# Score matmuls that read neighbouring columns and write PSUM with a step, and projections held to the second products of an attention and two-layer FFN kernel

## The chip, the cores and the metric

The kernel runs on one core of one Trainium2 chip. The metric is the time of the program on the device in microseconds (us), as the median of several runs.

## The reference, cut to what matters

```python
def _attn_ref(q, k, v):                       # (4, 8, 576, 64), fp32
    q_lm = q.reshape(B, H, 32, S // 32, D).mean(axis=3)   # 32 landmarks, each the mean of 18 rows
    k_lm = k.reshape(B, H, 32, S // 32, D).mean(axis=3)
    A = sm(q, k_lm); Bm = sm(q_lm, k_lm); C = sm(q_lm, k)  # softmaxes of scaled scores
    Z = ...                                   # six steps Z = 2 * Z - Z @ Bm @ Z
    return A @ Z @ C @ v

x = attention as (2304, 512)
h = x @ w_in;  g = h * tanh(softplus(h));  x = g @ w_out       # 512 -> 2048 -> 512
h = x @ w_in2; g = h * sigmoid(h);         return g @ w_out2
```

## The kernel before, in words

Attention is worked in eight groups of four heads (`Group`, two groups for each of the four batch elements, paired by `Pair`). A group loads q and k, turns them on TensorE into `tT["q"]` and `tT["k"]` (tiles `Tq` and `Tk`), and forms the landmarks `lmT`. Group 1 keeps its turned q and k in borrowed `wp` buffers, so its rows are named `wp`. Then `scores` (L1187) makes eight matmuls for k (called from `c_side`, L1237) and eight for q (called from `a_side`, L1304): fp32, 64 rows by 32 stationary columns, 288 moving columns, each into its own 32 partitions of one of two PSUM banks, so that eight small tiles of the array work at once. `tT` holds, for each partition, `[J2 = 9, HG = 4, LM = 32]`: the 32 columns of one head and one j lie side by side, and the next j of the head is 128 columns (512 bytes) on. The two calls read it in another order: q with j innermost (`p l j`), k with c innermost (`p w l c`, three j apart, 1,536 bytes), so that the scores come out in PSUM side by side in the order in which the softmax, the 32x32 transposes and the later products use them.

What comes out of a pair is `ut`, from C @ v and the six steps. With it, `projection(b, fb)` folds the attention's right side into `w_in`: eight fp32 matmuls of 512 columns (`t<-wa,ut`) into two `t` banks, from which ACT casts the high part `wp` and DVE subtracts for the low part. The first layer then is `emit_h` (first products, `h<-at,wp`, six matmuls of 288 columns into one of two `h` banks), `gated` (ACT takes Mish out of the `h` bank as `z`, casts `g`; DVE or POOL subtracts for its low part) and `emit_o` (second products, `y<-g,wo`, twelve matmuls). A product with fp32 exactness is three fp32r passes over high and low parts. The second layer (`second_layer`, 384 columns at a time, seven products where eight stood) follows.

The order of the instructions is made by the program itself before it runs: `Line` holds a model of the engines' times, chains such as `projections` are generators that yield the engine they wait for, and the main loop (L1575) takes the next `emit_o` or `emit_h` and lets due chains issue between their matmuls (`line.run()`). `projections` runs ahead of the first products as far as three `wp` buffers allow. `grown` (L1572) is 0 while groups are still being worked on, and 1 from the time all eight are done. Every engine then takes its instructions in the fixed order that results. Where the model finds TensorE idle before `grown`, the loop adds small transposes of `ident`.

Of the kernel before, what the change touches and what calls it, by code (L numbers as in the profile page):

```python
# [61 lines left out]
def f32(ap):  # L62
    return ap.bitcast(FP32)
# [347 lines left out]
def kernel(  # L411
# [15 lines left out]
    LM = 32  # L427
    J = S // LM
    J2 = J // 2
    SH = S // 2  # L430
    HG = 4
    GB = H // HG
    NG = B * GB
    VI = S // 96
    VC = 96 // LM
# [25 lines left out]
    def slots(n, of, **kw):  # L461
# [30 lines left out]
        out=twice.rearrange("p (a d) -> p a d", a=2),  # L492
# [18 lines left out]
    def until(cond):  # L511
        while not cond():
            yield "W"

    def marked(*m):
        return lambda: all(a in marks for a in m)
# [135 lines left out]
    t_r = Ring("t", ps_t, 2)  # L652
# [12 lines left out]
    def at_of(b):  # L665
        if b not in a_t:
            a_t[b] = at_p.tile([128, 2, GB, 2, SH], F32R, tag=f"at{b}", name=f"at{b}")
        return a_t[b]

    def projections():  # L670

        for half in range(2):
            for b in range(B):
                yield from until(marked(*((b, "ut", e) for e in range(GB))))
                for fb in (2 * half, 2 * half + 1):
                    yield from projection(b, fb)

    def projection(b, fb):
        keys = [("a", 0, fb * KD + kk) for kk in range(KD)]
        parts = 1 if fb or b else 2  # L680
        n = FB // parts
        yield from until(wp_r.any)
        for c in range(0, FB, n):
            done = [k if parts == 1 else (*k, c) for k in keys]
            yield from until(lambda: all(w_ready.get(k, LATE) <= line.now for k in done))
            yield from until(lambda: t_r.claim(GB))
            pp = [t_r.take([128, FB], FP32) for e in range(GB)]
            for i in range(HG):
                for e in range(GB):
                    r = slice(64 * ((i + e) % 2), 64 * ((i + e) % 2) + 64)  # L690
                    T.matmul(
                        out=pp[e][0][32 * i:32 * i + 32, 0:n],
                        lhsT=ut_t[b][r, e, i // 2, :],
                        rhs=f32(w_t[keys[2 * e + i // 2]])[r, c:c + n],
                        start=True,
                        stop=True,
                    )
            if not c:
                wp_ = wp_t[b, fb] = wp_r.take([128, 2, GB, FB], F32R)
                wp = wp_[0]  # L700
            yield "W"
            for e in range(GB):
                VA.copy(out=wp[:, 0, e, c:c + n], in_=pp[e][0][:, 0:n])
            yield "V"
            for e in range(GB):
                V.tensor_tensor(
                    out=wp[:, 1, e, c:c + n], in0=pp[e][0][:, 0:n], in1=f32(wp[:, 0, e, c:c + n]), op=ALU.subtract
                )
                Ring.give(pp[e])
            for f in range((fb * FB + c) // 128, (fb * FB + c + n) // 128):  # L710
                wp_ready[b, f] = line.end + 0.12 + SLACK
            yield "W"
        marks.add(("P", b, fb))
# [257 lines left out]
    def emit_h(ph, t, f):  # L971
        h = h_t[ph, t, f] = h_r.take([128, 512], FP32)
        n = tokens(ph, t)[1]
        b, e = divmod(t, 2)
        wp, at = wp_t[b, f // 4][0], a_t[b]
        ops = [(wp[:, i, k, f % 4 * 128:f % 4 * 128 + 128], at[:, j, k, e]) for k in range(GB) for i, j in PASSES]
        for i, (w, x) in enumerate(ops):
            T.matmul(out=h[0][:, :n], lhsT=w, rhs=x, start=(i == 0), stop=(i == len(ops) - 1))
            if i % STRIDE == STRIDE - 1:
                yield  # L980
# [126 lines left out]
    class Group:  # L1107
# [76 lines left out]
            yield "W"  # L1184
            marks.add((g, "T" + nm))

        def scores(self, i, mov):  # L1187
            s = [self.pairs.take([128, 512], FP32) for e in range(2)]
            for r in range(2):
                for h in range(HG):  # L1190
                    e = (h + r) % 2
                    T.matmul(
                        out=s[e][0][32 * h:32 * h + 32, 0:SH],
                        lhsT=self.lmT[64 * e:64 * e + 64, i, 32 * h:32 * h + 32],
                        rhs=mov(e, h),
                        start=True,
                        stop=True,
                    )
            return s, [x[0][:, 0:SH] for x in s]
# [37 lines left out]
        def c_side(self):  # L1237
            g = self.g
            yield from until(marked((g, "lmT"), (g, "Tk")))
            yield from until(lambda: self.pairs.open(2))  # L1240
            kT = self.tT["k"]
            s_, s_c = self.scores(
                1, lambda e, h: kT[64 * e:64 * e + 64, :, h, :].rearrange("p (c w) l -> p w l c", c=VC)
            )
            marks.add((g, "sc"))
            yield "V+"
            nm2 = s_p.tile([128, 2], FP32, tag="nm2", name="nm2")
            for e in range(2):
                V.tensor_reduce(out=nm2[:, e:e + 1], in_=s_c[e], axis=AX.X, op=ALU.max)
            yield "V"  # L1250
            nmc = s_p.tile([128, 1], FP32, tag="nmc", name="nmc")
            V.tensor_reduce(out=nmc, in_=nm2, axis=AX.X, op=ALU.max, negate=True)
            yield "A+"
            e_c = a_p.tile([128, 2, SH], FP32, tag="ec", name="ec", bufs=2)
            scr = s_p.tile([128, 1], FP32, tag="scr", name="scr")
            scm = s_p.tile([128, 1], FP32, tag="scm", name="scm")
            sc2 = s_p.tile([128, 2], FP32, tag="sc2", name="sc2")
            for e in range(2):
                A.activation(out=e_c[:, e], in_=s_c[e], func=ACTF.Exp, bias=nmc, accum_out=sc2[:, e:e + 1])
                Ring.give(s_[e])  # L1260
            line.add(self.total(scm, sc2, scr), self.kind("N"), "V", line.end + 0.17)
            yield "T+"
            yield from until(lambda: g == 0 or (g - 1, "cv") in marks)
            ect = a_p.tile([96, VI, 128], FP32, tag="ect", name="ect")
            for i0 in (0, 3):
                yield from until(self.banks.open)
                pe = self.banks.take([96, 3, 128], FP32)
                for i in range(i0, i0 + 3):
                    T.transpose(
                        out=pe[0][:, i - i0, :], in_=e_c[:, i % 2, 96 * (i // 2):96 * (i // 2) + 96], identity=ident  # L1270
                    )
                yield "W"
                VA.copy(out=ect[:, i0:i0 + 3, :], in_=pe[0])
                Ring.give(pe)
                yield "T+"
            yield from until(self.banks.open)
            pu_ = self.banks.take([128, D], FP32)
            pu = pu_[0]
            for i in range(VI):
                for h in range(HG):  # L1280
                    T.matmul(
                        out=pu[32 * h:32 * h + 32],
                        lhsT=ect[:, i, 32 * h:32 * h + 32],
                        rhs=self.vn[:, h, i, :],
                        start=(i == 0),
                        stop=(i == VI - 1),
                    )
            marks.add((g, "cv"))
            yield "V"
            yield from until(lambda: ("w", scr.name) in line.seen)  # L1290
            VAs.scaled(out=self.pair.yu[:, self.hg, LM:], in_=pu, scalar1=scr)
            Ring.give(pu_)
            yield "W"
            marks.add((g, "u"))
# [9 lines left out]
        def a_side(self):  # L1304
# [1 line left out]
            yield from until(marked((g, "lmT"), (g, "Tq"), (g, "sc")))  # L1306
            yield from until(lambda: self.pairs.open(2))
            qT = self.tT["q"]
            s_, s_a = self.scores(0, lambda e, h: qT[64 * e:64 * e + 64, :, h, :].rearrange("p j l -> p l j"))
            marks.add((g, "scores"))  # L1310
            if g == 1:
                for t_ in self.borrowed:
# [241 lines left out]
    line.add(attention(), "C")  # L1554
    line.add(loading(), "S")
    line.add(projections(), "X")
    line.add(inputs(), "S")
    line.add(summed(), "S")
# [7 lines left out]
    def o_time(u):  # L1566
        ph, t, f, first, last = u
        if first and not y_r.any_of(KD):
            return LATE
        return max(g_ready.get((ph, t, f), LATE), w_ready.get(("o", 0, f), LATE))  # L1570

    grown = 0  # L1572
    todo, flight = list(units), []
    idle = 0
    while todo or flight:  # L1575
        rank_decodes(*(flight[0] if flight else todo[0]))
        line.run()
        if not grown and marked(*((g, "done") for g in range(NG)))():

            grown = 1  # L1580
# [27 lines left out]
        to = o_time(flight[0]) if flight else LATE  # L1608
        th = h_time(todo[0]) if todo and len(flight) < FLIGHT else LATE
        if to <= line.now:  # L1610
            u = flight.pop(0)
            work = emit_o(*u)
        elif th <= line.now:
            u = todo.pop(0)
            flight.append(u)
            work = emit_h(*u[:3])
        else:
# [11 lines left out]
            assert idle < 20000, (line.now, todo[:1], flight[:1], [c[4].__name__ for c in line.chains], marks)  # L1629
            continue  # L1630
        idle = 0
        ph, t, f, first, last = u
        hs = work.__name__ == "emit_h"
        for _ in work:
# [54 lines left out]
```

## Time and profile before

| | us |
|---|---|
| median of 3 runs (lowest, highest) | 836.97 (835.3 to 837.58) |
| the profiled execution | 837.15 |
| its span, first to last instruction | 835.3 |
| TensorE matmuls busy | 811.0 |
| VectorE (DVE) busy | 557.7 |
| ScalarE (ACT) busy | 432.7 |
| GpSimd (POOL) busy | 114.5 |

The span is what the trace covers; 1.85 us of the profiled execution lie around it. Rows that read "t<-Tk,lmT x16" count two records for each fp32 matmul. In a timeline row the second number is the length from the first start to the last end of a merged run of instructions; matmuls are pipelined, so the next row starts before that end, and the step from one row's start to the next row's start is what a run occupies. The number in brackets is idle time of the engine just before the row and what ended it. Almost all operations are recorded at L262, the helper that issues them, so they are told apart by tiles.

### The profile page before, as it was taken

To read this page: it belongs to the slowest core of one execution; us is meant where nothing else is said; L and a number is where in the kernel's file an instruction comes from. 1 tells how busy PE (TensorE), PEld (TensorE's weight loads), DVE (VectorE), ACT (ScalarE), POOL (GpSimd) and SP (SyncE) were. 2 spreads that over 40 slices of the span, in tenths; PEclk is the share of its full clock that TensorE was granted. 3 is DMA by queue.
4 is the path that set the end of the run, shared out by engine and by line. 5 is a ranking of instruction groups with operands and counts; after the bars stand their busy time and mean duration, and the time that the engine had idled before them with its cause. 6 is when DMAs were issued, how large, how long until landed. Compare 5 with 4: busy or idle time off the path is not lost.

```text
span 835.3 us, 15167 instructions
## 1 busy us (share of the span) xinstructions
PE 811.0 (97%) x5866; PEld 722.3 (86%) x5866; DVE 557.7 (67%) x1192; ACT 432.7 (52%) x959; POOL 114.5 (14%) x157
## 2 busy tenths in 40 slices
PE   8799999999999999999998999999999999999997
PEld 6487888978989898989998888988888988988885
DVE  6978847647657698863638999677555567555542
ACT  4467636649556656452445655435544435544422
POOL 2000200201000001000001122211232211223210
PEclk9999999999999999999999999999999999999999
DMA  8875012311034645551125232102200000100002
GB/s 276 260 181 165 29 58 87 115 51 36 31 101 162 215 159 192 185 162 50 50 85 193 75 101 90 38 1 79 73 1 2 1 1 28 48 1 1 1 0 77
DMA packets 41736, 72.28 MB, mean 87 GB/s; under 512 B 3776, under 2 KB 31936, under 8 KB 41664
## 3 DMA queue, kind: packets, MB, share of 16 engines
q1 hardware_dynamic: 40768, 70.53, 26.5%
q8 instruction: 46, 0.75, 0.4%
q10 hardware_dynamic: 896, 0.79, 0.3%
q14 instruction: 26, 0.21, 0.1%
HBM read 57.15 MB, written 14.16 MB: 85 GB/s over the span
## 4 chain that ended last, share of the span: by engine, by line
PE 86%; DVE 6%; ACT 3%; DMA 2%; issue 1%; ACTq 0%; SPq 0%; DVEq 0%
PE y L262 47%; PE h L262 31%; PE t L262 8%; DMA wp<-in_q_dram 1%; ACT z L262 1%; DVE m L262 1%; DVE wa L262 1%; ACT L262 1%; ACT wp L262 1%; DVE at L262 1%; DMA wst<-in_moe_w_out_dram 1%; DVE wo L262 0%; ACT ec L262 0%; DVE bd L262 0%; DVE yu L262 0%
## 5 line engine op out<-in xcount | busy, mean ns | idle before, releaser
L262 PE MATMUL y<-g,wo 128*128 128x288 f32 x1536 | 226.1, 299 | 0.9 <-DVE g L262 0.9
L262 PEld LDWEIGHTS y<-g,wo 128*128 128x128 f32 x1536 | 208.3, 188 | 13.8 <-issue 11.7
L262 PE MATMUL y<-wo,xg 128*128 128x512 f32 x693 | 179.8, 394 | 0.0
L262 PEld LDWEIGHTS y<-wo,xg 128*128 128x128 f32 x693 | 128.4, 188 | 20.9
L262 DVE TENSOR_TENSOR z<-h,z 128x384 f32<-128x384 f32 x160 | 87.3, 555 | 70.4 <-PE h L262 68.0
L262 PE MATMUL h<-at,wp 128*128 128x288 f32 x768 | 122.8, 302 | 4.7 <-ACT z L262 4.0
L262 PEld LDWEIGHTS h<-at,wp 128*128 128x128 f32 x768 | 105.9, 188 | 17.6 <-issue 9.6
L262 ACT ACTIVATE z<-h 128x288 f32<-128x288 f32 x128 | 51.4, 415 | 55.9 <-PE h L262 55.4
L262 DVE TENSOR_TENSOR g<-z,g 128x288 fp32r<-128x288 f32 x121 | 53.9, 462 | 31.3 <-ACT g L262 28.2
L262 ACT ACTIVATE z<-z 128x384 f32<-128x384 f32 x93 | 48.9, 525 | 32.2 <-DVE z L262 32.0
L262 PE MATMUL h<-xg,wp 128*128 128x384 f32 x288 | 57.8, 335 | 0.0
L262 ACT CAST g<-z 128x288 fp32r<-128x288 f32 x122 | 50.9, 438 | 11.1 <-PE y L262 10.0
L262 PE MATMUL h<-xg,wf 128*128 128x384 f32 x282 | 56.5, 335 | 0.0
L262 DVE TENSOR_TENSOR xg<-z,xg 128x384 fp32r<-128x384 f32 x74 | 41.9, 566 | 20.1 <-ACT xg L262 20.0
L262 PEld LDWEIGHTS h<-xg,wp 128*128 128x128 f32 x288 | 51.3, 188 | 3.2
L262 PEld LDWEIGHTS h<-xg,wf 128*128 128x128 f32 x282 | 50.2, 188 | 3.1
L262 DVE SCALAR_TENSOR_TENSOR m<-wst,m 128x512 int32<-128x512 int32 x64 | 45.3, 712 | 0.7
L262 PE MATMUL y<-wo,wp 128*128 128x512 f32 x171 | 44.9, 394 | 0.0
L262 DVE TENSOR_TENSOR wp<-t,wp 128x512 fp32r<-128x512 f32 (+1 forms) x34 | 20.8, 654 | 28.7 <-ACT wp L262 28.7
L262 ACT CAST xg<-z 128x384 fp32r<-128x384 f32 x74 | 38.0, 513 | 1.6
L262 PEld LDWEIGHTS y<-wo,wp 128*128 128x128 f32 x171 | 31.7, 188 | 5.2
L262 POOL TENSOR_TENSOR g<-z,g 128x288 fp32r<-128x288 f32 x7 | 6.3, 898 | 216.3 <-ACT g L262 112.7
(227 smaller groups left out, 1137.2 us busy)
## 6 DMA issues: line engine op xcount, KB each, us to landing
wst<-in_moe_w_out_dram SPq DMA_DIRECT2D x32, 512.0 KB, 6.6
wst<-in_moe_w_in_dram SPq DMA_DIRECT2D x22, 512.0 KB, 5.5
kn<-in_k_dram SPq DMA_DIRECT2D x8, 576.0 KB, 5.6
vn<-in_v_dram SPq DMA_DIRECT2D x8, 576.0 KB, 7.0
yh<-ysb SPq DMA_DIRECT2D x32, 144.0 KB, 2.4
ysb<-yh SPq DMA_DIRECT2D x32, 144.0 KB, 2.7
ys<-ysb SPq DMA_DIRECT2D x32, 144.0 KB, 2.1
qn<-in_q_dram SPq DMA_DIRECT2D x7, 576.0 KB, 4.8
```

The lines of the kernel that those rows point to most:

```text
L262: r = getattr(self.nc[e], name)(**kw)
```

## The change

Two edits. First, both score calls read `tT` in its stored order, 32 neighbouring columns at a time, and `scores` gets a function `to` that gives the output the step that the read had: for k the columns land three floats apart (12 bytes), for q nine floats apart (36 bytes). The values and their places in PSUM are the same. Second, once `grown` is set, a projection may begin only while the unit of the main loop is an `emit_o`; the flag `between` is set for each unit before its matmuls are issued.

```diff
+    grown, between = 0, [False]
+
     def projections():
...
             yield from until(lambda: all(w_ready.get(k, LATE) <= line.now for k in done))
-            yield from until(lambda: t_r.claim(GB))
+            yield from until(lambda: (not grown or between[0]) and t_r.claim(GB))
...
-        def scores(self, i, mov):
+        def scores(self, i, mov, to):
...
-                        out=s[e][0][32 * h:32 * h + 32, 0:SH],
+                        out=to(s[e][0][32 * h:32 * h + 32, 0:SH]),
...
             s_, s_c = self.scores(
-                1, lambda e, h: kT[64 * e:64 * e + 64, :, h, :].rearrange("p (c w) l -> p w l c", c=VC)
+                1,
+                lambda e, h: kT[64 * e:64 * e + 64, :, h, :].rearrange("p (c w) l -> p c w l", c=VC),
+                lambda s: s.rearrange("p (w l c) -> p c w l", l=LM, c=VC),
             )
...
-            s_, s_a = self.scores(0, lambda e, h: qT[64 * e:64 * e + 64, :, h, :].rearrange("p j l -> p l j"))
+            s_, s_a = self.scores(
+                0, lambda e, h: qT[64 * e:64 * e + 64, :, h, :], lambda s: s.rearrange("p (l j) -> p j l", j=J2)
+            )
...
-    grown = 0
...
         idle = 0
+        between[0] = work.__name__ == "emit_o"
```

On TensorE, in the part of the program where a group's scores stand between products of the first layer (here group 4; `Tk` and `Tq` are the turned k and q), the difference of the two orders reads:

```order
-L262 MATMUL t<-Tk,lmT 32x288 x8
+L262 MATMUL t<-Tk,lmT 32x3x96 x8
 L262 MATMUL y<-g,wo 128x288 x20
 L262 MATMUL h<-at_1187,wp 128x288 x6
 L262 MATMUL y<-g,wo 128x288 x2
-L262 MATMUL t<-Tq,lmT 32x288 x8
+L262 MATMUL t<-Tq,lmT 32x9x32 x8
```

Nothing moved there; the output of the same matmuls now has two dimensions. Up to the end of the groups the two programs have the same matmuls in the same order on TensorE.

On TensorE after the last group, where the projections of batch element 2 (`ut_143`) and 3 (`ut_144`) stand among the first layer's products, the program before has:

```order
L262 MATMUL y<-g,wo 128x288 x36
L262 MATMUL h<-at_1187,wp 128x288 x8
L262 MATMUL t<-wa,ut_143 32x512 x8
L262 MATMUL h<-at_1187,wp 128x288 x22
L262 MATMUL y<-g,wo 128x288 x2
L262 MATMUL t<-wa,ut_144 32x512 x8
L262 MATMUL y<-g,wo 128x288 x58
```

and the changed one, at the same place:

```order
L262 MATMUL y<-g,wo 128x288 x36
L262 MATMUL h<-at_1187,wp 128x288 x30
L262 MATMUL y<-g,wo 128x288 x2
L262 MATMUL t<-wa,ut_143 32x512 x8
L262 MATMUL y<-g,wo 128x288 x22
L262 MATMUL t<-wa,ut_144 32x512 x8
L262 MATMUL y<-g,wo 128x288 x36
```

The projection that cut a run of 30 first products after 8 of them now stands after the run, two second products later, and the next one stands two units of second products behind it.

## Rows read from the trace of the kernel before

**Rows 1.** The page: busy by engine, and the last chain's shares.

```profile
PE 811.0 (97%) x5866; PEld 722.3 (86%) x5866; DVE 557.7 (67%) x1192; ACT 432.7 (52%) x959; POOL 114.5 (14%) x157
...
PE 86%; DVE 6%; ACT 3%; DMA 2%; issue 1%; ACTq 0%; SPq 0%; DVEq 0%
```

**Rows 2.** Stretches: start:end, length, PE, PEld, DVE, ACT, POOL busy, clock, DMA.

```profile
60.00:110.00 50.00, 48.77 (x514) 41.58 (x514) 42.77 (x99) 29.33 (x61) 6.21 (x7) 1.00 0.34 113
110.00:232.00 122.00, 119.48 (x1220) 102.47 (x1208) 73.86 (x187) 74.70 (x161) 11.81 (x14) 1.00 0.19 60
...
436.00:460.00 24.00, 21.43 (x142) 20.32 (x141) 18.72 (x41) 11.98 (x26) 3.14 (x4) 1.00 0.58 192
```

**Rows 3.** TensorE groups, shapes apart: count, busy us, mean ns of one.

```profile
L262 PE MATMUL t<-Tq,lmT 64*32 64x288 f32 x96 | 8.9, 760 | 0.0
...
L262 PE MATMUL t<-Tk,lmT 64*32 64x288 f32 x96 | 5.5, 500 | 0.0
...
L262 PE MATMUL t<-wa,ut 64*32 64x256 f32 x32 | 1.9, 388 | 0.4 <-ACT Tk L262 0.4
```

**Rows 4.** TensorE timeline around one group's scores: start, length, instruction.

```profile
123.01 0.88 PE L262 MATMUL t<-Tk,lmT 64*32 64x288 f32 x16
123.82 2.92 PE L262 MATMUL y<-g,wo 128*128 128x288 f32 x20
...
127.72 1.40 PE L262 MATMUL t<-Tq,lmT 64*32 64x288 f32 x16
129.06 1.19 PE L262 MATMUL y<-g,wo 128*128 128x288 f32 x7
```

**Rows 5.** TensorE timeline around a projection of 256 columns.

```profile
44.51 0.66 PE L262 MATMUL t<-wa,ut 64*32 64x256 f32 x16
45.10 1.09 PE L262 MATMUL y<-ident 128*128 128x128 f32 x8
```

**Rows 6.** TensorE timeline around two projections of 512 columns.

```profile
312.91 1.09 PE L262 MATMUL t<-wa,ut 64*32 64x512 f32 x16
313.93 0.81 PE L262 MATMUL h<-at,wp 128*128 128x288 f32 x4
315.53 2.67 PE L262 MATMUL h<-at,wp 128*128 128x288 f32 x18 [0.79 <-ACT z L262]
...
318.39 1.09 PE L262 MATMUL t<-wa,ut 64*32 64x512 f32 x16
319.41 1.87 PE L262 MATMUL y<-g,wo 128*128 128x288 f32 x12
```

**Rows 7.** ScalarE timeline at the first of these two.

```profile
314.09 1.07 ACT L262 CAST wp<-t 128x512 fp32r<-128x512 f32 x2 [2.45 <-PE t L262]
315.05 0.73 ACT L262 ACTIVATE z<-h 128x288 f32<-128x288 f32 x2
```

**Rows 8.** Waits of TensorE from 225 to 460: us in total, times, longest.

```profile
PE h L262 <- ACT z L262: 3.2, 5, 0.8
PE h L262 <- DVE z L262: 1.4, 1, 1.4
```

**Rows 9.** TensorE timeline, three other places of the first of these waits.

```profile
285.68 1.58 PE L262 MATMUL h<-at,wp 128*128 128x288 f32 x10 [0.54 <-ACT z L262]
...
372.36 1.84 PE L262 MATMUL h<-at,wp 128*128 128x288 f32 x12 [0.29 <-ACT z L262]
...
400.17 2.00 PE L262 MATMUL h<-at,wp 128*128 128x288 f32 x13 [0.80 <-ACT z L262]
```

**Rows 10.** Chain of work from 36 to 42, by line.

```profile
by line: DVE wa L262 56.1%; DVE m L262 15.6%; PE t L262 12.8%; DVE at L262 6.3%; DVE wp L262 5.7%; issue 4.2%
```

**Rows 11.** Waits of VectorE from 12 to 36: us in total, times, longest.

```profile
DVE nm L262 <- PE y L262: 1.5, 2, 1.0
```

**Rows 12.** Chain of work by line, 60 to 110, then 110 to 232.

```profile
by line: PE y L262 29.5%; PE t L262 29.2%; PE h L262 10.5%; ACT L262 5.8%; DVE wo L262 4.9%; DVE m L262 3.5%; issue 2.6%; DVE wp L262 2.4%; ACT m L262 2.3%; DVE bd L262 1.8%; ACT z L262 1.7%; DVE a_t L262 1.4%; ACT at L262 1.4%; ACT eb L262
...
by line: PE y L262 38.8%; PE t L262 28.4%; PE h L262 16.6%; ACT L262 2.1%; DVE lmk L262 1.9%; DVE lmq L262 1.9%; issue 1.7%; DVE nm L262 1.4%; DVE bd L262 1.2%; DVE at L262 1.1%; ACT ec L262 1.1%; ACT wp L262 0.9%; DVE g L262 0.8%; ACT z L2
```

## The prediction

> **What bounds the kernel now.** I read the page first. TensorE is busy for 97% of the span and carries 86% of the chain that ended last [rows 1], so a microsecond taken from TensorE can reach the end, but only in stretches where TensorE does not then wait for another engine. So I cut the span into stretches and looked at the chain of waits in each. From 110 to 232 TensorE is idle for 122 - 119.5 = 2.5 us, and its three tiles (y, t, h) carry 38.8 + 28.4 + 16.6 = 84% of the chain [rows 2, 12]. From 60 to 110 VectorE is busy for 42.8 of 50 us and TensorE's share of the chain is 29.5 + 29.2 + 10.5 = 69% [rows 2, 12]. Before that the chain is VectorE's: from 36 to 42 its decoding of weights (wa, m) alone is 72%, TensorE 13% [rows 10]. After 225 TensorE's waits are few and have a pattern, 3.2 us in five waits of first products for ScalarE's z [rows 8].
>
> **Edit one, the scores: what they cost now.** Each of the eight groups issues one batch for k and one for q, eight matmuls (16 records) each. The reader should compare two batches of equal work: from its start to the next row's start k occupies 123.82 - 123.01 = 0.81 us, q 129.06 - 127.72 = 1.34 us [rows 4]. Single records differ likewise, 500 ns against 760 [rows 3]. The columns, the tile shapes and the output are alike; what differs is the order in which the moving operand is read. So reading order costs time here.
>
> What such a batch takes when the read is side by side and the write too is shown by the projections, which use the same 64x32 tiles, 16 records: 256 columns occupy 45.10 - 44.51 = 0.59 us [rows 5], 512 columns 313.93 - 312.91 = 1.02 us [rows 6]. For 288 columns that gives, as an estimate between these rows, 0.59 + (32/256) x 0.43 = 0.64 us. If the stepped write is free, a k batch gains 0.81 - 0.64 = 0.17, a q batch 1.34 - 0.64 = 0.70, a group 0.87, and eight groups 7.0 us.
>
> **What the write with a step costs** no row shows: every TensorE row of before writes neighbouring columns. The bounds: from below nothing, since 0.64 us is already the rate of matmuls that read and write side by side, and a stepped write has nothing less to do. From above, the widest step on a read that the trace has: a batch of 1.34 us for both. I take nothing, being the nearer to the rows: a k read whose step is three times q's (1,536 against 512 bytes) costs only a quarter of what q's does (0.17 against 0.70), so a step is not dear by its width alone, and the steps of the writes are 12 and 36 bytes.
>
> The Trainium skill, "PSUM — Partial Sum Buffer", section "Specifications (TRN2)", speaks against the edit: it gives PSUM lines of 8 bytes and says that any non-contiguous access pattern slows matmuls significantly. No run shows this yet; by it the gain of the scores would shrink, vanish or turn round. It is weighed as a rival.
>
> **How much of the 7.0 us reaches the end.** Groups 4 to 7 have their scores after 110, where I pass on TensorE's 84% of the chain: 4 x 0.87 x 0.84 = 2.9. Groups 2 and 3 have theirs before it: 2 x 0.87 x 0.69 = 1.2. Groups 0 and 1 come first, ahead of a stretch that VectorE's queue bounds; between nothing (its queue is full anyway) and the 1.5 us that VectorE waited there for the score banks to take their maximum (nm) [rows 11]. I take 0.8, the middle. Sum 4.9 us, 70% of 7.0. Nothing else is issued: matmuls, their count, the filler transposes and the readers' patterns stay, so no transfer or cast is added.
>
> **Edit two, the projections.** Ten projections start after 225; six of them cut a run of first products. What the cut does is read at 313 [rows 6, 7]: ScalarE's queue is in order, and the two casts of wp, planned there, wait for the projection's last matmul until 314.09 and then take 0.96 us; the Mish of an h bank stands behind them at 315.05, and as there are only two h banks, TensorE stands idle 0.79 us before its next first products. The same occurs at 285 and 400 [rows 9] and once more between them: of the 3.2 us in five waits [rows 8], 0.29 at 372 [rows 9] follows no projection closely, and I expect one of its kind to stay. Removed: 3.2 - 0.3 = 2.9 us. The projection itself costs the same between second products: 319.41 - 318.39 = 1.02 us against 1.02 in the h run [rows 6]. Where the casts wait now, TensorE has 22 to 58 second products of at most 0.15 us each to do (20 of them take 2.92 us [rows 4]), some 3 to 8 us against the 0.96 us of casts, so no h bank is needed in that time. The cover ends where, as once in the new order, a projection stands right before first products; then up to 0.8 us returns. I charge 0.3 and count 2.6 us. Later projections make wp later, by about 3 us, but a wp made when a buffer comes free is first read eight units later, and a unit is 18 products of that length, so some 20 us: hidden.
>
> Sum: 837.15 - 4.9 - 2.6 = 829.65 on the profiled execution, which stands 0.18 above the median: **829.5 us**.
>
> **The rivals.**
> *Absorbed.* The scores gain less because the step costs a little or VectorE does not follow. A batch of 0.90 us for both saves 2.15 - 1.80 = 0.35 a group, 8 x 0.35 x 0.70 = 2.0, with the projections 4.6: 832.4. For it speaks VectorE's 86% from 60 to 110 [rows 2]; against it the small idle time of TensorE after 110. VectorE absorbing groups 0 to 3 altogether leaves 2.9 + 2.6 = 5.5: 831.5.
> *The step costs as much as q's read did.* Both batches 1.34 us: k loses 0.53, q gains nothing, 8 x 0.53 x 0.70 = 3.0 lost, 2.6 won by the projections: 837.4, no change. For it speaks that a step on the read, of whatever width, cost something in both orders; against it, that the steps here are 14 times narrower and more than those. By the rule of the Trainium skill quoted above this rival or the next is what happens; no run shows it yet.
> *The step costs more, slower.* Twice q's excess on both batches, 0.64 + 1.40 = 2.04 us: 8 x (4.08 - 2.15) x 0.70 = 10.8 lost, less 2.6: 845. It becomes slower than no change can explain when 8 x 0.70 x (two batches - 2.15) exceeds 2.6 + 2.5, that is from 1.53 us a batch on. For it speaks that no row has such a write; against it, that the write would then cost 1.53 - 0.64 = 0.89 us a batch, more than the 0.70 of the dearest read.
> *The projections bring nothing.* The casts now stand ahead of second products' g casts or another z, and waits of the same size come back: 837.15 - 4.9 = 832.3 or, with one VectorE wait more at the change of layers (1.4 us at 458 now [rows 8], in a stretch where VectorE is busy 18.7 of 24 us [rows 2]), 833.6. The order of that stretch is replanned too, and its 24 - 21.4 = 2.6 us of idle TensorE may shift either way by 1 to 2 us; I add nothing.
>
> **How the numbers follow.** No change can be told apart within about 0.3%, 2.5 us: 834.5 to 839.5. Forecast as above, 826 to 831.4: 0.50. Absorbed, 831.4 to 834.5: 0.22. Projections without effect: 0.05. Step as dear as q's read, 834.5 to 839.5: 0.14. Step dearer: 0.09. The most that could be won is 7.0 + 2.9 + the 1.4 at 458 = 11.3, 825.9. So faster 0.76, same 0.15, slower 0.09. The range takes the first three cases and the better half of the fourth: 825.9 to 837.
>
> **What the profile of the changed kernel would show.** Right, if k and q batches both step by about 0.64 us and their records last near 410 ns (500 less half of the k batch's 170); if first products wait for z after 225 once at most, under 0.5 us in all; and if TensorE's idle time from 60 to 232 stays under 6 us. The step is dear if q's record does not fall clearly under k's old 500 ns, or if k's rises. Absorbed, if batches fall as said and TensorE's waits for VectorE between 60 and 110 grow by over 1 us. The forecast falls altogether with a batch over 1.1 us, or with waits of more than 2 us that stand behind the moved casts or at the change of layers.

## The result and the profile after

| | before | after |
|---|---|---|
| median of 5 runs (lowest, highest), us | 836.97 (835.3 to 837.6) | 827.56 (825.96 to 828.59) |
| after / before, 95% interval | | 0.9887 (0.9868 to 0.9906) |
| the profiled execution, its span, us | 837.15, 835.3 | 827.56, 825.6 |

The change makes the kernel 1.13% faster, about 9.4 us; 829.5 was predicted, 825.9 to 837 as the range. Beside the experiments below the kernel before ran 27 times more, with medians of 836.14 to 836.20; measured on those, the gain is about 8.6 us. The page of the changed kernel says, in its list of engines:

```profile
PE 803.1 (97%) x5866; PEld 723.1 (88%) x5866; DVE 556.8 (67%) x1194; ACT 430.6 (52%) x956; POOL 117.1 (14%) x158
```

TensorE has the same 5866 instructions and 7.9 us less to do [rows 1]. By shape (count, busy us, mean ns of one) the score records are now alike:

```profile
L262 PE MATMUL t<-Tq,lmT 64*32 64x288 f32 x96 | 4.8, 415 | 0.0
...
L262 PE MATMUL t<-Tk,lmT 64*32 64x288 f32 x96 | 4.6, 415 | 0.0
```

They were 760 and 500 [rows 3]. TensorE's timeline at the same group's two batches:

```profile
118.46 0.72 PE L262 MATMUL t<-Tk,lmT 64*32 64x288 f32 x16
119.10 2.89 PE L262 MATMUL y<-g,wo 128*128 128x288 f32 x20
...
122.98 0.71 PE L262 MATMUL t<-Tq,lmT 64*32 64x288 f32 x16
123.62 1.58 PE L262 MATMUL y<-g,wo 128*128 128x288 f32 x10
```

From start to next start both take 0.64 us, where [rows 4] has 0.81 and 1.34. In the stretches (length, busy time of PE, PEld, DVE, ACT and POOL, granted clock, DMA) TensorE's idle time from 60 to 232 is 1.40 + 3.17 = 4.57 us, and was 1.23 + 2.52 = 3.75 [rows 2]:

```profile
60.00:110.00 50.00, 48.60 (x517) 41.85 (x515) 41.06 (x96) 29.55 (x62) 6.21 (x7) 1.00 0.27 91
110.00:232.00 122.00, 118.83 (x1239) 104.47 (x1238) 77.08 (x195) 78.08 (x169) 11.69 (x14) 1.00 0.19 60
...
436.00:460.00 24.00, 22.15 (x119) 20.99 (x118) 22.04 (x48) 14.63 (x31) 4.38 (x6) 0.93 0.35 116
```

The last of these rows has something that the kernel before did not have there: a granted clock under 1.00. It comes back below. Where the two projections stood at 313 and 318 [rows 6], the changed kernel has:

```profile
304.97 4.48 PE L262 MATMUL h<-at,wp 128*128 128x288 f32 x30
309.29 0.43 PE L262 MATMUL y<-g,wo 128*128 128x288 f32 x2
309.65 1.09 PE L262 MATMUL t<-wa,ut 64*32 64x512 f32 x16
310.67 3.21 PE L262 MATMUL y<-g,wo 128*128 128x288 f32 x22
313.81 1.09 PE L262 MATMUL t<-wa,ut 64*32 64x512 f32 x16
314.82 5.07 PE L262 MATMUL y<-g,wo 128*128 128x288 f32 x36
```

No bracket, so no wait that the trace shows. A projection still occupies 1.02 and 1.01 us. TensorE's waits from 225 to 460 (total, times, longest) are now:

```profile
PE h L262 <- DVE z L262: 1.9, 1, 1.9
PE h L262 <- ACT z L262: 1.8, 3, 1.0
```

Five waits for ScalarE's z have become three, 3.2 us have become 1.8; the wait for VectorE's z at the change of layers has grown from 1.4 to 1.9 [rows 8].

To see where the 9.7 us of span went I read, in each trace, the starts of four instructions: the first scores of k; the last small product of the groups (`t<-bd,yu`); the first product of the second layer (`h<-x,wf`); the third product of the second layer that reads `x`. The table gives the first of them and then the time from each to the next, the last column to the end of the span:

| us | first scores | to the groups' end | to the second layer | change of layers | rest |
|---|---|---|---|---|---|
| before | 12.91 | 217.12 | 220.47 | 25.14 | 359.66 |
| after | 11.79 | 210.86 | 216.68 | 26.65 | 359.62 |
| difference | 1.12 | 6.26 | 3.79 | -1.51 | 0.04 |

The first 1.12 us are not the change's: the load of group 1's q landed 8.35 us after its issue in the one trace and 7.23 us in the other, and over all ten kernels of this study, with the old scores or the new, the first scores start anywhere from 11.7 to 13.0. In this execution the two edits bring 6.26 and 3.79, and at the change of layers this execution lost 1.51 us again.

### The profile page after: what moved, and what is told of

Its sections match the earlier page's. It is cut to its first block, busy times and chain, and to the rows that moved or that the text cites. A ratio compares the mean times of both kernels' runs of the same rounds, so it can differ in the third digit from the quotient of the medians.

```text
span 825.6 us, 15175 instructions
## 1 busy us (share of the span) xinstructions
PE 803.1 (97%) x5866; PEld 723.1 (88%) x5866; DVE 556.8 (67%) x1194; ACT 430.6 (52%) x956; POOL 117.1 (14%) x158
## 4 chain that ended last, share of the span: by engine, by line
PE 86%; DVE 5%; ACT 3%; DMA 3%; issue 2%; ACTq 0%; SPq 0%
PE y L262 47%; PE h L262 32%; PE t L262 8%; DMA wst<-in_moe_w_out_dram 1%; DMA wp<-in_q_dram 1%; DVE wa L262 1%; ACT L262 1%; DVE at L262 1%; ACT z L262 1%; DMA wst<-in_moe_w_in_dram 0%; DVE wo L262 0%; DVE bd L262 0%; DVE yu L262 0%; DVE z L262 0%; DVE m L262 0%
## 5 line engine op out<-in xcount | busy, mean ns | idle before, releaser
L262 DVE TENSOR_TENSOR z<-h,z 128x384 f32<-128x384 f32 x166 | 90.6, 555 | 70.5 <-PE h L262 68.2
L262 PE MATMUL h<-at,wp 128*128 128x288 f32 x768 | 120.8, 301 | 3.1 <-ACT z L262 2.9
L262 DVE TENSOR_TENSOR g<-z,g 128x288 fp32r<-128x288 f32 x122 | 56.5, 476 | 39.1 <-ACT g L262 34.5
L262 ACT ACTIVATE z<-z 128x384 f32<-128x384 f32 x96 | 50.4, 526 | 35.5 <-DVE z L262 35.3
L262 POOL TENSOR_TENSOR wo<-m,wo 128x512 fp32r<-128x512 f32 x7 | 9.5, 1356 | 182.0 <-ACT wo L262 92.4
```

What stands on the lines that cost most here:

```text
L262: r = getattr(self.nc[e], name)(**kw)
```

## The experiments

**Either edit alone.** The first kernel has the new scores and lets projections begin anywhere.

```diff
-            yield from until(lambda: (not grown or between[0]) and t_r.claim(GB))
+            yield from until(lambda: t_r.claim(GB))
```

> The first edit alone: scores read neighbours and write with a step, projections start where they did before. Theory (both edits work and add, scores larger): batches of 0.64 us for k and for q, the groups end some 6.3 us earlier than before counted from the first scores, and the five waits of first products for z after 225 stay, so 830 to 831.5 us. Rival (the scores' gain is mostly absorbed and the gain seen with both edits came from the replanned order after 230): 833 us or more.

Measured: 830.53 us, 0.9928 of before (0.9915 to 0.9940). To the groups' end 212.30 us, to the second layer 220.15, change of layers 25.09. TensorE's waits after 225 are those of before [rows 8], but for a shorter one for VectorE's g:

```profile
PE h L262 <- ACT z L262: 3.2, 5, 0.8
PE h L262 <- DVE z L262: 1.4, 1, 1.4
PE y L262 <- DVE g L262: 0.6, 1, 0.6
```

That last wait was, in the kernel before:

```profile
PE y L262 <- DVE g L262: 0.9, 1, 0.9
```

So after the groups the scores bring no more than those 0.3 us (220.15 against 220.47), and nearly all of their gain comes before. The first part is 1.44 us longer than the 210.86 of the changed kernel, although the matmuls and their order are the same up to there. Of this 1.22 us were lost before the first pair of groups ended, where TensorE stood still twice without a cause that the trace shows (0.48 us before 20.71, 0.90 before 28.93). After that, from 35.3 to 38.7, the granted clock was 0.50, but it cost nothing there, because TensorE has to wait for VectorE at this place anyway:

```profile
40.24 0.55 PE L262 MATMUL t<-ident,kn 128*128 128x128 f32 x3 [0.62 <-DVE wp L262]
```

The wait in brackets is 1.23 us in the changed kernel, whose clock stayed at 1.00 there. From the pair's last small products to this instruction all ten kernels of this study take 5.82 or 5.83 us, the three in which the clock fell and the seven in which it did not.

The second kernel has the old scores and the new rule for projections.

```diff
-                lambda e, h: kT[64 * e:64 * e + 64, :, h, :].rearrange("p (c w) l -> p c w l", c=VC),
-                lambda s: s.rearrange("p (w l c) -> p c w l", l=LM, c=VC),
+                lambda e, h: kT[64 * e:64 * e + 64, :, h, :].rearrange("p (c w) l -> p w l c", c=VC), lambda s: s
...
-                0, lambda e, h: qT[64 * e:64 * e + 64, :, h, :], lambda s: s.rearrange("p (l j) -> p j l", j=J2)
+                0, lambda e, h: qT[64 * e:64 * e + 64, :, h, :].rearrange("p j l -> p l j"), lambda s: s
```

> The second edit alone: projections only between second products after the groups are done, scores as before. Theory (a wait costs more than its idle time, and some 1.5 us of the second edit's gain are lost again to a lower clock at the change of layers): TensorE reaches the second layer 3 to 4 us earlier than before, in all 833 to 835.5 us. Rival (the second edit brings 1 us or less, the forecast's rival of projections without effect): 836 us or more. If the clock falls here too at the first products of the second layer, the fall belongs to the new order and not to the faster scores.

Measured: 834.13 us, 0.9973 of before (0.9963 to 0.9983). To the groups' end 217.17 us, as before; to the second layer 217.23, 3.24 less; change of layers 26.66, 1.52 more. So that loss does not need the faster scores. TensorE's timeline there, and the stretch behind it:

```profile
455.41 2.05 PE L262 MATMUL h<-x,wp 128*128 128x384 f32 x6 [1.84 <-DVE z L262]
457.26 2.07 PE L262 MATMUL h<-xg,wf 128*128 128x384 f32 x6
```

```profile
457.00:460.00 3.00, 3.00 (x12) 2.87 (x11) 2.48 (x8) 2.85 (x7) 0.00 (x0) 0.65 0.00 0
```

The gains of the two alone, 0.72% and 0.27%, add up to 0.99%; both together gave 1.13%, with an interval that holds 0.99. The edits act in different stretches and do not need each other.

The longer wait of 1.84 us comes with the new order of the projections (the scores alone have 1.42), and behind it the granted clock is low. The next experiment bears on that as well.

**Is the step of the write free, or only this narrow one?** The reads stay side by side; each group's outputs get a step of their own, from 1 to 144 floats.

```diff
+STEPS = ((3, 9), (3, 9), (1, 2), (4, 8), (16, 32), (48, 72), (96, 144), (3, 9))
...
-                lambda s: s.rearrange("p (w l c) -> p c w l", l=LM, c=VC),
+                lambda s: s.rearrange("p (x s) -> p s x", s=STEPS[g][0])
...
-                lambda s: s.rearrange("p (l j) -> p j l", j=J2)
+                lambda s: s.rearrange("p (x s) -> p s x", s=STEPS[g][1])
```

> The changed kernel, with the scores of groups 2 to 6 written to PSUM at other steps: k and q of group 2 at 1 and 2 columns, group 3 at 4 and 8, group 4 at 16 and 32, group 5 at 48 and 72, group 6 at 96 and 144 (4 to 576 bytes); the read is of 32 neighbours throughout. The scores of these groups then stand permuted in their banks, so that part of the computation is other than the reference's. Theory (a step on an fp32 write to PSUM costs nothing at any width): every batch 0.64 to 0.65 us, step 1 too. Rival (a wide step is dear, and 12 and 36 bytes were below the point from which it is): batches from some step on rise above 0.75 us.

Measured: 827.22 us in a single run. TensorE's timeline for q of group 5 (step 72, 288 bytes) and k of group 6 (step 96, 384 bytes):

```profile
147.72 0.72 PE L262 MATMUL t<-Tq,lmT 64*32 64x288 f32 x16
148.37 1.84 PE L262 MATMUL y<-g,wo 128*128 128x288 f32 x12
...
179.42 0.72 PE L262 MATMUL t<-Tk,lmT 64*32 64x288 f32 x16
180.06 3.18 PE L262 MATMUL y<-g,wo 128*128 128x288 f32 x22
```

0.65 and 0.64 us. Steps of 1, 2, 16, 32 and 48 floats take 0.64 to 0.65 too; 144 takes 0.70 at a place where the changed kernel's step of 9 takes 0.70, and group 3, where the changed kernel's batches take 0.90 and 1.13, has 0.86 and 1.13 with steps of 4 and 8. For these matmuls the step is free from 8 to 576 bytes.

This execution shows something else too, at the change of layers:

```profile
449.96 1.32 PE L262 MATMUL h<-x,wp 128*128 128x384 f32 x6 [1.84 <-DVE z L262]
451.12 1.20 PE L262 MATMUL h<-xg,wf 128*128 128x384 f32 x6
```

The wait is the changed kernel's, but the products behind it take 1.16 and 1.05 us, the clock stays at 1.00, and the change of layers takes 25.09 us, as in the kernel before. The low clock is thus no fixed part of the new order.

**What in the read costs?** Here the writes are side by side, and the reading order differs by group: the two old orders exchanged between q and k (group 2); for k three columns that lie 512 bytes apart instead of 1,536 (group 3); runs of 2, 4, 8, 16 and 32 neighbours (groups 3 to 5).

```diff
-                lambda e, h: kT[64 * e:64 * e + 64, :, h, :].rearrange("p (c w) l -> p c w l", c=VC),
-                lambda s: s.rearrange("p (w l c) -> p c w l", l=LM, c=VC),
+                lambda e, h: kT[64 * e:64 * e + 64, :, h, :].rearrange(READS[g][0][0], **READS[g][0][1]), lambda s: s
...
-                0, lambda e, h: qT[64 * e:64 * e + 64, :, h, :], lambda s: s.rearrange("p (l j) -> p j l", j=J2)
+                0, lambda e, h: qT[64 * e:64 * e + 64, :, h, :].rearrange(READS[g][1][0], **READS[g][1][1]), lambda s: s
```

> The kernel with the second edit, scores written side by side, and the read order changed by group: group 2 reads k in q's old order (nine columns 512 bytes apart) and q in k's old order (three columns 1,536 bytes apart), group 3 k in an order of three columns 512 bytes apart and q in runs of 2 neighbours, group 4 in runs of 4 and 8, group 5 in runs of 16 and 32. The scores of these groups then stand permuted in their banks, so that part of the computation is other than the reference's. Theory (the read order sets the price, by how many far columns come round before a neighbour of the first is read, not by the step's width): k in q's order 1.34, q in k's order 0.81, three at 512 bytes also 0.81, runs of 4 and more near 0.64. Rival (the price belongs to the operand or the step's width): group 2 keeps 0.81 for k and 1.34 for q, or three columns at 512 bytes cost nearer to 1.34.

Measured: 832.91 us in a single run. The records by tile (shortest, median and longest in ns, first and last start in us): k in q's old order, q in k's old order, k with three columns 512 bytes apart, runs of 2, runs of 4.

```profile
L262 PE MATMUL t<-Tk,lmT x16: 753/762/770, 53.9 to 54.5; 64*32 64x288 f32 x16
...
L262 PE MATMUL t<-Tq,lmT x16: 492/500/510, 59.4 to 59.8; 64*32 64x288 f32 x16
...
L262 PE MATMUL t<-Tk,lmT x16: 492/500/508, 77.9 to 78.6; 64*32 64x288 f32 x16
L262 PE MATMUL t<-Tq,lmT x16: 402/428/467, 82.2 to 83.0; 64*32 64x288 f32 x16
...
L262 PE MATMUL t<-Tk,lmT x16: 402/415/427, 122.3 to 122.7; 64*32 64x288 f32 x16
```

The price goes with the order, not with the operand: k costs 762 in q's order and q 500 in k's. It does not go with the width of the step: three columns 512 bytes apart cost 500, as three 1,536 bytes apart do, while nine columns 512 bytes apart cost 762. With runs of two neighbours 428 is left, and with four or more the 415 of the changed kernel.

**Do wider outputs pay for a step?** The group's other fp32 TensorE work, the transposes and landmark sums of 128 columns by 128 rows, gets stepped outputs of 1 to 64 floats.

```diff
+TSTEPS = (1, 1, 2, 8, 4, 16, 32, 64)
...
-                        out=pt[0][:, i, :],
+                        out=pt[0][:, i, :].rearrange("p (x s) -> p s x", s=TSTEPS[g]),
...
-                            out=pl[0][:, i, :],
+                            out=pl[0][:, i, :].rearrange("p (x s) -> p s x", s=TSTEPS[g]),
```

> The changed kernel, with matmuls on the whole array written with a step: the transposes of k and q (fp32, 128 columns, three in a row) at 2 columns in group 2, 8 in group 3, 4, 16, 32 and 64 in groups 4 to 7, and in groups 2 and 3 the landmark sums (fp32, 128 columns, eighteen records) at 2 and 8. Turned q and k then stand permuted, so that part of the computation is other than the reference's. Theory (a step on an fp32 write costs nothing on the whole array either): three transposes keep their 0.24 us from start to start and eighteen landmark records their 2.0 us at every step. Rival (eight small tiles hid it, each writing a quarter of the partitions): transposes, which pass their columns once, rise with the step, to 0.4 us or more.

Measured: 828.13 us in a single run. TensorE's timeline in group 7, with a step of 64 floats (256 bytes):

```profile
203.39 0.49 PE L262 MATMUL t<-ident,qn 128*128 128x128 f32 x3
203.63 0.51 PE L262 MATMUL h<-at,wp 128*128 128x288 f32 x2
```

Three transposes take 0.24 us, as with a step of 8 floats in group 3 (59.56 to 59.80) and one of 2 in group 2 (41.34 to 41.58); the 18 landmark records of group 3, with a step of 8, take 2.01 us as in the changed kernel. All of this is fp32 work: an fp32r product with a stepped output was not tried.

**What was lost at the change of layers?** If the clock falls because TensorE stands idle there, filler products in the gap should hold it up, and win 1 to 1.5 us. Eight matmuls of 384 columns were put ahead of the last of the second layer's first seven products, just before the gap, into a bank that this product overwrites afterwards; then, in another kernel, four.

```diff
+            for i in range(FILLERS if t == turn == 0 and name == "22" else 0):
+                T.matmul(out=bank[0][:, 0:TH], lhsT=w_[0][:, 0, 0:128], rhs=x[:, 0, 0], start=True, stop=True)
```

> The changed kernel with eight more matmuls of 384 columns ahead of the last of the first seven products of the second layer, into a bank that the product then overwrites; results as before. They stand in the time in which TensorE waits for VectorE's z (1.85 us). Theory (the clock fell at 449 because TensorE stood idle there, and the 1.5 us lost to it are saved when it is busy): clock 1.00 at the following products, 0.7 to 1.6 us faster than the changed kernel, 826 to 827. Rival (the wait does not shrink and the eight delay what VectorE waits for): the wait for z stays above 1 us after them and the time is that of the changed kernel or 1 us more.

Measured with eight: 827.26 us, 0.9893 of before (0.9878 to 0.9908). The timeline at the gap and the stretch behind it:

```profile
449.72 1.32 PE L262 MATMUL h<-x,wp 128*128 128x384 f32 x6 [0.94 <-DVE z L262]
```

```profile
449.00:452.00 3.00, 2.28 (x13) 2.28 (x14) 2.97 (x9) 2.30 (x6) 0.73 (x1) 1.00 0.02 6
```

The clock stays at 1.00, and the change of layers takes 25.57 us against 26.65. But the time is that of the changed kernel, and the kernels with other steps of the write and with full-width steps, without a filler, have the wait (1.84 and 1.85), a clock of 1.00 and 25.09 and 25.10 us. That the fillers held the clock is therefore not shown.

> As the kernel with eight added matmuls ahead of the last of the second layer's first seven products, but with four (0.7 us); results as before. With eight, the wait for z had moved 0.47 us later, so that 1.08 of the 1.5 us lost to the lower clock were won in its trace. Theory (four are enough to keep the clock and delay z less): clock 1.00 at the following products, from the first matmul of the second layer to the third x product 25.1 to 25.3 us against 26.65 in the changed kernel and 25.57 with eight, 826 to 826.8 us. Rival (the clock falls again, since TensorE still stands idle over 1 us): 26 us or more over that stretch, 827.5 us.

Measured with four: 827.74 us, 0.9896 of before (0.9879 to 0.9912); change of layers 25.60. The stretch behind the gap, and one much earlier in the same execution:

```profile
36.00:38.00 2.00, 2.00 (x19) 0.67 (x18) 2.00 (x7) 1.34 (x4) 0.00 (x0) 0.50 0.82 326
...
451.00:453.00 2.00, 2.00 (x12) 2.00 (x13) 1.97 (x6) 2.00 (x6) 0.16 (x1) 1.00 0.00 0
```

The clock stays up at the change of layers again, with a wait of 1.63 left, and falls near 36, where it costs nothing (see the scores alone). The 826 to 826.8 that I expected did not come. My theory that the fall is a standing cost of the new order, to be won back, has fallen: the fall comes in some executions only, and fillers bring nothing that can be measured.

**The rule for projections from the start on.** It now holds while groups are being worked on too, and forbids only first products.

```diff
-    grown, between = 0, [False]
+    grown, between = 0, [True]
...
-            yield from until(lambda: (not grown or between[0]) and t_r.claim(GB))
+            yield from until(lambda: between[0] and t_r.claim(GB))
...
-        between[0] = work.__name__ == "emit_o"
+        between[0] = work.__name__ != "emit_h"
```

> The changed kernel with the rule of the second edit from the start on: while groups are still worked on, a projection may not begin during first products either. Theory (each wait for z behind a projection's casts costs its idle time and more): the two such waits between 110 and 225, 0.8 us of idle time together, go, 826 to 827 us. Rival (before the end of the groups the first products need their wp at once, so a held projection delays them and the replanned order brings new idle time): the same as the changed kernel or slower, up to 832.

Measured: 827.04 us, 0.9886 of before (0.9869 to 0.9902): the changed kernel's time. The groups end 2.74 us later (213.60 against 210.86), with waits between 40 and 225 that the changed kernel does not have there:

```profile
PE t L262 <- ACT ec L262: 1.7, 2, 0.9
PE t L262 <- POOL lmq L262: 1.3, 1, 1.3
```

2.29 us of that come back before the second layer (214.39 against 216.68), and the change of layers takes 25.11 with a wait of 1.43, so nothing is gained or lost in all. Moving projections away from first products among the groups goes with new waits of the groups themselves; why these arise was not followed up.

## Why the prediction was right, step by step

**What a batch costs.** 0.64 us was worked out from two projections, and 0.64 was measured for k and for q; the records of "near 410" last 415. With 1.34 + 0.81 - 2 x 0.64 = 0.87 a group and 7.0 in all, TensorE's own saving came as predicted (6.8 over all batches as they stand in the two traces).

**The step of the write is free.** The prediction chose nothing between nothing and 0.70, because a k read with three times the step cost a quarter of q's price. The choice was right, and that width is not what costs is shown for writes by the third experiment and for reads by the fourth. But this reason did not lead to nothing: a step on the read had cost something in both orders, and no row had a step on a write. That the price was nothing, and not some part of 0.70, was luck. The Trainium skill, "PSUM — Partial Sum Buffer", "Specifications (TRN2)", has any non-contiguous pattern slow matmuls significantly, which spoke for the rivals at 837.4 and 845. The runs here do not bear it out for fp32 matmuls in small tiles at any step from 8 to 576 bytes, nor for fp32 transposes from 8 to 256; the measurement decides. The same skill's "Advanced Engine Details and Errata", "SBUF Cachelines", gives lines of 16 bytes in SBUF and wants at least two hits on a line for full performance: 428 ns with runs of two, 3% over the 415 from four neighbours on, comes near it, but it gives no reason why nine far columns in turn should cost 762 and three 500.

**How much reaches the end: mis-sized, 4.9 for 6.26 in the profiled execution.** I multiplied the gain by TensorE's share of the chain. Between the ends of the pairs of groups the gains were 1.77, 1.64, 1.17 and 1.68 us, of 1.74 each; the prediction had 0.8 for the first pair, 1.2 for the second and 2.9 for the last two together, which came to 2.85. So 90% arrived in this execution, not 70%. A share of the chain tells how much of a stretch an engine holds, not how much of a cut at one place arrives. In groups 0 and 1 TensorE held little of the chain (28% from 12 to 36), but the scores themselves, which are written to `y` banks there, stood on it. The chain of the kernel before has them here (start, length):

```profile
12.77 2.24 PE y L262 x32
...
17.68 1.90 PE y L262 x27
```

and that of the changed kernel, with two filler transposes in the first row:

```profile
11.64 1.35 PE y L262 x34
...
15.67 0.63 PE y L262 x13
```

VectorE's waits for these scores (nm) fell from 1.5 [rows 11] to 0.9 us, and all of the cut arrived. "Absorbed" did not occur: TensorE's idle time from 60 to 110 grew by 0.17 us, and its one larger wait after 110, for VectorE's `at` at 128, from 0.87 to 1.52, is where the third pair lost its part.

**The projections: mis-sized, 2.6 for 3.79, by errors of both signs.** The removed waits were priced at their idle time. A run of first products with a projection and a wait in it cost more than that: 30 of them at 311.75 in the kernel before took, without the projection's 1.02, 5.26 us with one wait of 0.79; at the same place, 304.97, the changed kernel's 30 take 4.32, and runs of 30 without a bracket take 3.96 to 4.36 in both kernels. That is 0.9 to 1.3 us for 0.79. On the other side, new waits came that the prediction had at "once at most, under 0.5 us": three, 0.42, 1.00 and 0.35 us. The longest, on TensorE and on ScalarE:

```profile
267.80 1.76 PE L262 MATMUL h<-at,wp 128*128 128x288 f32 x12
270.56 2.64 PE L262 MATMUL h<-at,wp 128*128 128x288 f32 x18 [1.00 <-ACT z L262]
273.04 4.91 PE L262 MATMUL y<-g,wo 128*128 128x288 f32 x36
```

```profile
269.54 0.66 ACT L262 ACTIVATE wa<-wst 128x512 f32<-128x512 f32 x1 [6.83 <-DMA wst<-in_moe_w_in_dram]
270.11 0.70 ACT L262 ACTIVATE z<-h 128x288 f32<-128x288 f32 x2
```

The z stands in ScalarE's queue behind the decoding of a weight that waits for its transfer: not the casts of `wp` that the prediction looked at, but the same mechanism. These 30 products take 5.24 us, 0.9 to 1.3 more than runs without a bracket. From the groups' end to the second layer both traces have the same matmuls. The 498 first products took 73.33 us from start to next start and now take 69.76: their idle time fell by 1.45 (3.22 to 1.77), the rest by 2.13. The 1011 second products took 136.57 and now take 136.35: a wait of 0.89 us among them is gone, but the rest grew by 0.67. The projection itself costs 1.02 us at either place, as predicted, but its neighbours pay too: 22 second products behind one take 3.14 us (310.67), 143 ns each, 36 without one 4.79, 133 ns each. So 2.34 of the 3.79 won is idle time; the other 1.45, which is 2.13 less 0.67, the trace does not put down to a wait.

**The change of layers: nothing added, and 1.51 us lost in the profiled execution.** "Its 24 - 21.4 = 2.6 us of idle TensorE may shift either way by 1 to 2 us" has the size, but by luck, since it is not idle time that was lost: from the second layer's first product to the end of TensorE's wait for z it takes 9.34 us in the kernel before and 9.32 in the changed one, although the wait grew by 0.41. The loss lies behind the wait. TensorE's timeline there, and the stretches:

```profile
448.65 2.14 PE L262 MATMUL h<-x,wp 128*128 128x384 f32 x6 [1.85 <-DVE z L262]
450.59 1.98 PE L262 MATMUL h<-xg,wf 128*128 128x384 f32 x6
452.40 1.55 PE L262 MATMUL y<-wo,xg 128*128 128x512 f32 x6
```

```profile
446.00:449.00 3.00, 1.15 (x7) 0.83 (x6) 3.00 (x7) 0.40 (x2) 1.63 (x2) 0.97 0.56 175
449.00:452.00 3.00, 3.00 (x11) 3.00 (x10) 2.53 (x7) 2.76 (x8) 0.00 (x0) 0.50 0.00 0
452.00:455.00 3.00, 3.00 (x16) 2.74 (x15) 2.40 (x7) 2.47 (x6) 0.00 (x0) 0.96 0.00 0
```

After a wait of 1.85 us the granted clock is 0.50, which is 1.2 of 2.4 GHz, for about three microseconds. The two products that fall into it take 1.94 and 1.81 us from start to start, where the kernel before had 1.16 and 1.06: 1.5 us, the whole loss. Of the five kernels with a wait of 1.84 or 1.85 here, the clock fell in three profiled executions (the changed kernel, the projections alone, the reading orders) and not in two (both steps of writes). Adding nothing was right for an execution without the fall: 25.09 and 25.10 against 25.14. How often it falls in the timed runs can't be read from their times.

**The sum.** Predicted 4.9 + 2.6 = 7.5; measured 6.26 + 3.79 - 1.51 = 8.5 in the span, and 1.1 us of chance with the first load on top in the profiled execution. So of the 2.1 us by which this execution lies under its forecast of 829.65, one is the two terms that were too small, less the loss, and one is luck with a load that no term had. The sizes of the terms are one execution's too. The kernels with the new scores and the same order up to the groups' end take 210.86 to 212.30 us for that part, a gain of 4.8 to 6.3; those with the changed kernel's order of projections behind the groups take 216.45 to 217.63 for the next, a gain of 2.8 to 4.0. The changed kernel's execution is the best of six in the first and second of seven in the next. The forecast's 4.9 lies at the lower end of what occurs, and its 2.6 just under it. (The chances were added up slightly wrong: the cases that end faster make 0.77, the case of no change 0.14.)

## What to carry to other kernels

If a matmul must permute its columns, let the write do it and read in runs of four or more neighbours: the write's step cost nothing here in fp32, the read's up to 0.70 of 1.34 us. What a cut brings is asked at its place, by whether that instruction stands on the chain or the next engine waits for it, not by an engine's share of a long stretch. Before moving work in front of an in-order engine, look for everything that can hold its queue, transfers included, since the waits of 0.79 and 1.00 us taken apart here cost 0.9 to 1.3 us each.

## What the hardware showed that was not expected

- The step of an fp32 write into PSUM was free from 8 to 576 bytes in tiles of 64 by 32 (0.64 to 0.65 us a batch), and from 8 to 256 bytes in transposes of 128 by 128 (0.24 us for three).
- The price of a read out of order depends on how many far columns come in turn before a neighbour does, 415 ns a record for runs of four or more, 428 for runs of two, 500 for three far columns, 762 for nine, and not on how far they lie. Why is open.
- The granted clock falls to 0.50 for some microseconds in some executions and not in others with the same instructions and the same wait. At the change of layers it fell after a wait of 1.84 or 1.85 us in three profiled executions of five, and after 1.63 or less in none of five. Near 36, behind a wait of 1.64 us for VectorE that every kernel has, it fell in three of ten (the scores alone, the projections alone, four fillers). What decides is open.
- What such a fall costs depends on who waits: 1.5 us at the change of layers, nothing near 36, where TensorE's next wait for VectorE was shorter by what it had lost (0.3 to 0.6 us instead of 1.2).
- A lower mean clock did not go with a longer time from run to run: of the 13 runs of the kernel before that lie beside the two single edits, the five at 0.996 have a median of 835.88 us, the eight at 0.998 and 0.999 one of 836.32. Of the five runs of the changed kernel the two at 0.995 and 0.996 are the slowest, 828.57 and 828.59 against 825.96 to 827.56, which is too few to tell. A stretch's loss to the clock in one trace is no loss of the median until timed runs show it.
